# A fused attention and bilinear feed-forward kernel: another PSUM bank for the tail-tail scores in four slots, value products right behind them, and later key transposes

## Chip, cores, metric

One Trainium2 chip (trn2), one core. The metric is the device time of one execution in microseconds (us); lower is better. The runs of one kernel lie within 0.1 to 0.75 per cent of each other; differences below one per cent are therefore judged by traces as well as by times. All runs told here are fast, at a granted TensorE clock of 0.994 to 1.0.

## The reference

Attention with a relative position bias for 8 batches of 8 heads (576 positions, 64 wide); its output is the input of a bilinear feed-forward network of width 1536.

```python
def attn(q, k, v, bias_table):               # q, k, v: (8, 8, 576, 64)
    scores = q @ k.T / 8 + bias_table[bucket(|i - j|)]
    return softmax(scores) @ v
def ffn(x, w_a, w_b, w_out):                 # x: (4608, 512), w_a, w_b: (512, 1536)
    return ((x @ w_a) * (x @ w_b)) @ w_out
```

## The kernel before

The kernel schedules by hand. It works in slots: slot `s` computes the scores of one pair of heads and, beside it, the value products of pair `s - 1` and some "units" of the feed-forward part: `a` and `b` (one 128x512 block of `x @ w_a` or `x @ w_b`) and `o` (output). The 576 positions are 4 blocks of 128 and a tail of 64, so there are main scores, tail scores (`qkt`) and tail-tail scores (`qktt`). PSUM has eight banks: four for scores, one each named AV and TR, and a ring of two named FF.

```python
    ps_av = ctx.enter_context(tc.tile_pool(name="ps_av", bufs=1, space=bass.MemoryType.PSUM))
    ps_tr = ctx.enter_context(tc.tile_pool(name="ps_tr", bufs=1, space=bass.MemoryType.PSUM))
    ps_ff = ctx.enter_context(tc.tile_pool(name="ps_ff", bufs=2, space=bass.MemoryType.PSUM))
    ...
    def qk_tail(p):                                        # TensorE: qkt, then qktt
        ...
        pt = bank(AV if wide(p) else TR, FP32, f"qktt{p}")
        ...
    def ex_tail(p):                                        # ScalarE: exp of qktt, then of qkt
    def run(s, us):          # main scores of slot s and four units, as two half-array streams;
        ...                  # the units' banks: FF and AV, then FF and TR
    def put_in(us, where):   # a plain unit: 4 matmuls, then its eviction
        ...                  # an 'a' ends on ScalarE (L544), a 'b' with a product on VectorE (L548)
    def turns(s):                                          # transposes by DMA, for the next batch
        b = s // 4 + 1
        if 2 < b < B and s % 4 < 3:
            turn(b, "qkt"[s % 4])                          # queries, keys, then the tails QTt and KTt
    ...
            # slots from 9 on; o = output units, rest = plain 'a' and 'b' units
            first = o[0:1] or rest[0:1]
            rest = rest if o else rest[1:]
            steps += [lambda: run(s, four), lambda: qk_tail(s), lambda: put_in(first, FF), lambda: ex_tail(s),
                      lambda: mul(s, 0)] + TQ + X(o[1:2]) + [lambda: mul(s, 1)]
            steps += TK + X(o[2:]) if o else []
            steps += [A(0, 1, 2), N(0)]                    # value products in AV, normalisation
            steps += [] if o else TK
            steps += X(rest[0:1]) + [lambda: mul(s, 2), A(3, 4), N(3), lambda: t_x(s - 1), lambda: turns(s)]
            steps += X(rest[1:2]) + [lambda: mul(s, 3), lambda: mul_tail(s)]
```

`mul` is the multiplication by the exponentials of the bias (VectorE), `N` the normalisation (VectorE), `TQ` and `TK` are transposes on TensorE with their copies out on VectorE.

The softmax here doesn't subtract the row's maximum and nothing guards it: scores larger than these inputs give would overflow.

Of the kernel before, what the change touches and what calls it, by code (L numbers as in the profile page):

```python
# [13 lines left out]
def kernel(  # L14
# [12 lines left out]
    FP32 = mybir.dt.float32  # L27
# [92 lines left out]
    def wide(p):  # L120
        return p >= R4
# [158 lines left out]
    TR = (ps_tr, "tr")  # L280
# [3 lines left out]
    def bank(where, dt, name):  # L284
        return where[0].tile([128, 512 if dt is FP32 else 1024], dt, tag=where[1], name=name)
# [65 lines left out]
    def qk(p, t0):  # L351
        qk1(p, t0)
        qk1(p, t0 + 1)

    def ex(p, t):
        ps = st[p]["ps", t]
        at = atp.tile([128, 2, SM], BF16, tag="at", name=f"at{p}_{t}")
        nc.scalar.activation(out=at[:, :, :], in_=ps[:, :, :], func=ACTF.Exp, scale=scale)  # L358
        st[p]["at", t] = at

    def mul(p, t):
        at, w = st[p]["at", t], W_sb[p % 4]
        lo, hi = max(0, 128 * (t - 1)), min(SM, 128 * (t + 2))
        y = 383 - (lo - 128 * (t - 1))
        z = y - (hi - lo)
        nc.vector.tensor_tensor(out=at[:, :, lo:hi], in0=at[:, :, lo:hi],  # L366
                                in1=w[:, :, y:(None if z < 0 else z):-1], op=MULT)

    def qk_tail(p):
        ps = ps_sc.tile([128, 2, 512], FP32, tag="sc", name=f"qkt{p}")  # L370
        if wide(p):
            for t in range(NM):
                for hh in range(2):
                    r = slice(64 * hh, 64 * hh + 64)
                    nc.tensor.matmul(out=ps[:, hh, ST * t:ST * t + ST], lhsT=kT_(p, t)[r, :],  # L375
                                     rhs=qTt_(p)[r, ST * hh:ST * hh + ST], start=True, stop=True)
            for x in range(2):
                nc.tensor.matmul(out=ps[:, x, 256:512], lhsT=kTt_(p), rhs=qT_(p)[:, 2 * x:2 * x + 2, :],  # L378
                                 start=True, stop=True)
        for t in range(NM if not wide(p) else 0):  # L380
            nc.tensor.matmul(
                out=ps[:, 0, :].rearrange("p (h t c) -> p h t c", h=2, t=NM)[:, :, t, :],
                lhsT=kT_(p, t), rhs=qTt_(p), start=True, stop=True)
        if not wide(p):
            nc.tensor.matmul(out=ps[:, 1, :], lhsT=kTt_(p), rhs=qT_(p), start=True, stop=True)
        pt = bank(AV if wide(p) else TR, FP32, f"qktt{p}")
        for hh in range(2):
            nc.tensor.matmul(out=pt[:, 0:ST], lhsT=kTt_(p), rhs=qTt_(p)[:, ST * hh:ST * hh + ST],
                             start=(hh == 0), stop=(hh == 1))
        st[p]["ps"] = (ps, pt)  # L390

    def ex_tail(p):
        ps, pt = st[p]["ps"]
        at = att_sb[p % 2]
        nc.scalar.activation(out=at[:, 1024:1024 + ST], in_=pt[:, 0:ST], func=ACTF.Exp, scale=scale)  # L395
        if not wide(p):
            nc.scalar.activation(out=at[:, 0:1024].rearrange("p (a x) -> p a x", a=2),
                                 in_=ps[:, :, :], func=ACTF.Exp, scale=scale)
        else:
            nc.scalar.activation(out=at[:, 0:1024].rearrange("p (y a x) -> p a y x", y=2, a=2),  # L400
                                 in_=ps[:, :, :].rearrange("p a (y x) -> p a y x", y=2),
                                 func=ACTF.Exp, scale=scale)
# [218 lines left out]
    def put_in(us, where):  # L621
        nonlocal here
        for u in us:
            here = where
            for x in u_mms(u):
                mm(x)
            here = None
            u_end(u)
# [21 lines left out]
    def run(s, us):  # L650
        u, v_ = [sorted(x, reverse=True) for x in (us[0:2], us[2:4])]
        u, v_ = list(zip(u, (FF, AV))), list(zip(v_, (FF, TR)))
        qk1(s, 0)
        ex(s, 0)
        got0 = begin(*u)
        qk1(s, 1)
        ex(s, 1)
        got1 = begin(*v_)
        qk1(s, 2)
        ex(s, 2)  # L660
        end(*u, got0)
        qk1(s, 3)
        ex(s, 3)
        end(*v_, got1)
# [156 lines left out]
    def turns(s):  # L821
        b = s // 4 + 1
        if 2 < b < B and s % 4 < 3:
            turn(b, "qkt"[s % 4])
# [12 lines left out]
    for s in range(4, NP + 1):  # L837
        new = s < NP
        U = "unit"
        A = lambda *jq: (lambda: [av(s - 1, j, AV if j < 3 or s == NP else TR) for j in jq])  # L840
        N = lambda j: (lambda: norm(s - 1, j))
        steps = []
        if s == 4:
            steps += [U, U, lambda: qk1(4, 0), lambda: ex(4, 0), lambda: qk1(4, 1), U, lambda: ex(4, 1),
                      lambda: qk1(4, 2), U, lambda: ex(4, 2), lambda: qk1(4, 3), lambda: ex(4, 3),
                      lambda: mul(4, 0), U, tails4, U, lambda: qk_tail(4), lambda: ex_tail(4),
                      lambda: mul(4, 1), U, lambda: mul(4, 2), U, lambda: mul(4, 3),
                      lambda: mul_tail(4), U, lambda: t_q(5, TR), lambda: c_q(5), U,
                      lambda: t_k(5, AV), lambda: c_k(5), U, U]
        elif new and s >= R4:  # L850
            e = early((s + 1) // 4)
            n_in, n_out = plan.get(s, (6, 3))
            four, rest, o = take(ins, 4), take(ins, n_in - 4), take(outs, n_out)
            X = lambda us: [lambda: put_in(us, FF)]
            TQ = [lambda: t_q(s + 1, TR), lambda: c_q(s + 1)] if e else []
            TK = [lambda: t_k(s + 1, TR), lambda: c_k(s + 1)] if e else []
            first = o[0:1] or rest[0:1]
            rest = rest if o else rest[1:]
            steps += [lambda: run(s, four), lambda: qk_tail(s), lambda: put_in(first, FF), lambda: ex_tail(s),
                      lambda: mul(s, 0)] + TQ + X(o[1:2]) + [lambda: mul(s, 1)]  # L860
            steps += TK + X(o[2:]) if o else []
            steps += [A(0, 1, 2), N(0)]
            steps += [] if o else TK
            steps += X(rest[0:1]) + [lambda: mul(s, 2), A(3, 4), N(3), lambda: t_x(s - 1), lambda: turns(s)]
            steps += X(rest[1:2]) + [lambda: mul(s, 3), lambda: mul_tail(s)]
        elif new:
            X1 = [lambda: t_x(s - 1, TR), lambda: c_x(s - 1), lambda: turns(s)]
            steps += [lambda: qk(s, 0), lambda: ex(s, 0), U, lambda: ex(s, 1), A(0, 1, 2), N(0), U,
                      lambda: mul(s, 0), A(3, 4), N(3), U, lambda: mul(s, 1)]
            steps += X1 if s == R4 - 1 else []  # L870
            steps += [lambda: qk(s, 2), lambda: ex(s, 2), U, lambda: t_q(s + 1, TR), lambda: c_q(s + 1),
                      lambda: ex(s, 3), U, lambda: mul(s, 2), lambda: t_k(s + 1, AV), lambda: c_k(s + 1),
                      U, lambda: mul(s, 3), lambda: qk_tail(s), lambda: ex_tail(s), U]
            steps += X1 if s < R4 - 1 else []
            steps += [U, lambda: mul_tail(s), U]
        else:
            steps += [U, A(0, 1, 2), N(0), U, U, A(3, 4), N(3), U, U, lambda: t_x(s - 1, AV),
                      lambda: c_x(s - 1), U, U, U, U]
        quota = quotas.get(s, 9)
        if s == NP:  # L880
            ring3 = True
            c = ins[0][1]
            units = [u for u in outs if u[1] < c] + [u for u in ins if u[1] == c]
            units += [u for u in outs if u[1] == c]
            for d in range(c + 1, NCH):
                units += [u for x in (ins, outs) for u in x if u[1] == d]
            nxt = 0
        seen, put = 0, 0
        nu = sum(1 for x in steps if x is U)
        for x in steps:  # L890
            if x is U:
                seen += 1
                n = (quota * seen + nu - 1) // nu - put
                put_units(n)
                put += n
            else:
                x()
        b = s // 4 + 1
        if new and s % 4 == 2 and b + 1 < B:
            load_qkt(b + 1)  # L900
        if new and 2 <= b < B:
            if s % 4 == 0:
                load_v(b)
                if b % 2 == 0:
                    load_vt(b, 2)
# [31 lines left out]
```

## Time and profile before

| | before |
|---|---|
| median of 3 runs at first, 4 with one beside the changed kernel | 414.95 us, 414.91 us |
| span of the profiled run | 413.9 us |
| TensorE busy | 399.2 us, 96% |
| TensorE start to start, 512 columns | 0.216 us |

How to read it: a core whose TensorE is busy nearly throughout gains only where TensorE stands still, so all that follows is about gaps of 0.1 to 1 us between matmul starts. The prediction shows those lines. "Lost" below always means: the start of a matmul, less the start of the one before it, less what that one costs (columns / 2.4 plus 2.5 ns, which fits the 0.216 us and, for 128 and 65 columns, the 0.056 and 0.029 of this trace). One more view of the kernel before matters for what came: the tile KTt, the transposed tail keys of the next batch, from the query by tile.

```profile
L378 PE MATMUL qkt<-QTb,KTt x2: 272/278/283, 114.8 to 114.9; 128*128 128x256 bf16 x2
...
L331 SPq DMA_TRANSPOSE KTt<-ktl x1: 1371/1371/1371, 106.7 to 106.7; - x1
...
DMA to landing us min/median/max: 6.2/6.2/6.2
```

The transpose was issued at 106.71 us and landed at 112.86; its reader, the tail scores of slot 12, started at 114.83. In this trace there were 2 us to spare.

### The profile page before, as it was taken

To read this page: it belongs to the slowest core of one execution; us is meant where nothing else is said; L and a number is where in the kernel's file an instruction comes from. 1 tells how busy PE (TensorE), PEld (TensorE's weight loads), DVE (VectorE), ACT (ScalarE), POOL (GpSimd) and SP (SyncE) were. 2 spreads that over 40 slices of the span, in tenths; PEclk is the share of its full clock that TensorE was granted. 3 is DMA by queue.
4 is the path that set the end of the run, shared out by engine and by line. 5 is a ranking of instruction groups with operands and counts; after the bars stand their busy time and mean duration, and the time that the engine had idled before them with its cause. 6 is when DMAs were issued, how large, how long until landed. Compare 5 with 4: busy or idle time off the path is not lost.

```text
span 413.9 us, 9454 instructions
## 1 busy us (share of the span) xinstructions
PE 399.2 (96%) x3831; PEld 218.9 (53%) x3890; DVE 201.0 (49%) x531; ACT 244.0 (59%) x345; POOL 119.6 (29%) x161
## 2 busy tenths in 40 slices
PE   8799999999999999999999999999999999999996
PEld 3574555566656555555555555555555544444443
DVE  4685666656465444644455455555544330430330
ACT  4997476676887666766666666666666222322321
POOL 9897848904455006600550030000000000000000
PEclk9999999999999999999999999999999999999999
DMA  9999999999979939992899249421111202002004
GB/s 159 189 155 178 158 159 150 180 147 125 140 54 169 164 47 85 152 143 63 78 170 145 64 61 122 92 65 42 35 35 41 65 2 102 2 0 102 2 1 101
DMA packets 164940, 40.83 MB, mean 99 GB/s; under 512 B 155320, under 2 KB 160224, under 8 KB 164896
## 3 DMA queue, kind: packets, MB, share of 16 engines
q0 software_dynamic: 110448, 18.75, 63.9%
q1 hardware_dynamic: 53168, 21.03, 27.7%
q8 instruction: 30, 0.49, 0.5%
q10 hardware_dynamic: 1280, 0.43, 0.5%
q14 instruction: 14, 0.11, 0.1%
HBM read 38.77 MB, written 9.45 MB: 116 GB/s over the span
## 4 chain that ended last, share of the span: by engine, by line
PE 82%; DMA 10%; POOL 4%; issue 2%; DVE 1%; ACT 1%; POOLq 0%; DVEq 0%
PE pa L538 21%; PE po L538 21%; PE pb L538 20%; PE av L432 7%; PE qk L347 6%; DMA wb<-in_moe_w_b_dram 4%; DMA kn<-in_k_dram 4%; PE av L423 2%; DMA vm<-in_v_dram 2%; PE qkt L378 2%; PE qkt L375 1%; PE po L555 1%; POOL qn L134 1%; POOL kn L134 1%; DVE XG L469 1%
## 5 line engine op out<-in xcount | busy, mean ns | idle before, releaser
L538 PE MATMUL pb<-xn,wb 64*128 64x512 bf16 (+1 forms) x592 | 156.6, 377 | 1.3
L538 PE MATMUL pa<-xn,wa 128*128 128x512 bf16 (+1 forms) x609 | 157.2, 377 | 0.7 <-DVE XG L469 0.3
L358 ACT ACTIVATE at<-qk 128x1024 bf16<-128x1024 f32 x128 | 129.3, 1026 | 38.6 <-PE qk L347 36.3
L544 ACT ACTIVATE ha<-pa 128x512 f32<-128x512 f32 x108 | 64.8, 600 | 61.8 <-PE pa L538 60.7
L538 PEld LDWEIGHTS <-wa 64*128 64x128 bf16 (+1 forms) x616 | 56.6, 96 | 44.3 <-DVE XG L469 2.3
L538 PEld LDWEIGHTS <-wb 64*128 64x128 bf16 (+1 forms) x616 | 56.8, 96 | 41.1 <-issue 1.5
L548 DVE TENSOR_TENSOR g<-pb,ha 128x512 bf16<-128x512 f32 x60 | 41.5, 692 | 65.5 <-PE pb L538 38.3
L366 DVE TENSOR_TENSOR at<-at,W 128x512 bf16<-128x512 bf16 (+1 forms) x128 | 59.4, 483 | 2.3 <-DMA W<-bias_tab 2.1
L128 POOL DMA_DIRECT2D vm<-in_v_dram x32 | 28.2, 918 | 95.1 <-PE av L432 83.5
L573 ACT ACTIVATE ob<-po 128x512 f32<-128x512 f32 x35 | 20.9, 598 | 55.6 <-PE po L538 53.6
L538 PE MATMUL po<-wo,g 128*128 128x512 bf16 x216 | 51.8, 379 | 0.6
L432 PEld LDWEIGHTS <-at 128*128 128x128 bf16 x992 | 39.3, 97 | 8.7 <-issue 3.3
L432 PE MATMUL av<-vm,at 128*128 128x65 bf16 x992 | 42.9, 193 | 0.0
L548 DVE TENSOR_TENSOR q<-pb,ha 128x512 bf16<-128x512 f32 x32 | 22.1, 692 | 41.8 <-ACT ha L544 21.0
L423 PE MATMUL av<-vt,att 128*128 128x130 bf16 x156 | 34.6, 222 | 2.3 <-ACT att L395 2.2
L538 PEld LDWEIGHTS <-g 128*128 128x128 bf16 x228 | 21.5, 98 | 22.9 <-issue 0.7
L468 DVE RECIPROCAL rc<-av 128x6 f32<-128x6 f32 x64 | 12.1, 188 | 44.1 <-PE av L432 43.5
L469 DVE TENSOR_TENSOR XG<-av,rc 128x384 bf16<-128x384 f32 x64 | 31.4, 491 | 2.2
L347 PE MATMUL qk<-QTb,KTb 64*128 64x512 bf16 x160 | 32.0, 379 | 0.0
L128 POOL DMA_DIRECT2D qn<-in_q_dram x28 | 24.3, 911 | 21.7 <-PE trq L296 14.3
L538 PE MATMUL po<-wo,q 128*128 128x512 bf16 x116 | 29.6, 379 | 0.6
L128 POOL DMA_DIRECT2D kn<-in_k_dram x28 | 24.4, 914 | 3.4 <-DMA wb<-in_moe_w_b_dram 1.8
(133 smaller groups left out, 349.2 us busy)
## 6 DMA issues: line engine op xcount, KB each, us to landing
out_dram<-ob SPq DMA_DIRECT2D x32, 256.0 KB, 2.3
vm<-in_v_dram POOLq DMA_DIRECT2D x28, 128.0 KB, 5.5
qn<-in_q_dram POOLq DMA_DIRECT2D x24, 128.0 KB, 8.0
kn<-in_k_dram POOLq DMA_DIRECT2D x24, 128.0 KB, 8.3
wa<-in_moe_w_a_dram POOLq DMA_DIRECT2D x3, 512.0 KB, 7.4
wb<-in_moe_w_b_dram POOLq DMA_DIRECT2D x3, 512.0 KB, 9.5
wo<-in_moe_w_out_dram POOLq DMA_DIRECT2D x1, 1536.0 KB, 13.3
W<-bias_tab POOLq DMA_DIRECT2D x4, 192.0 KB, 5.6
```

Source lines behind the costliest of these rows:

```text
L128: nc.gpsimd.dma_start(out=(vm[b % 2][:, h0:h1, t, 0:Dh] if dst is None else dst[b % 2][:, :].rearrange("p (t h d) -> p t h d", h=H, t=NM)[ ...
L347: nc.tensor.matmul(out=ps[:, hh, :], lhsT=kT_(p, t)[r, :], rhs=qT[r, :, :], start=True, stop=True)
L358: nc.scalar.activation(out=at[:, :, :], in_=ps[:, :, :], func=ACTF.Exp, scale=scale)
L366: nc.vector.tensor_tensor(out=at[:, :, lo:hi], in0=at[:, :, lo:hi], in1=w[:, :, y:(None if z < 0 else z):-1], op=MULT)
L423: nc.tensor.matmul(out=pav[:, slot, :, :], lhsT=x, rhs=vt[b // 2 % 2][:, 4 * i + hp, :, 0:Dh + 1], start=fresh, stop=True, skip_group_chec ...
L432: nc.tensor.matmul(out=pav[:, slot, hh, :], lhsT=x, rhs=vm[i][:, 2 * hp + hh, t, 0:Dh + 1], start=False, stop=True, skip_group_check=True)
L468: nc.vector.reciprocal(out=rc, in_=pav[:, 0:n, :, Dh])
L469: nc.vector.tensor_tensor(out=xg[:, j0:j0 + n, :, :], in0=pav[:, 0:n, :, 0:Dh], in1=rc.unsqueeze(3).to_broadcast([128, n, 2, Dh]), op=MULT)
L538: return nc.tensor.matmul(out=o[:, :], lhsT=w[r, :], rhs=m[r, :], start=first if start is None else start, stop=final if stop is None else ...
L544: nc.scalar.activation(out=ha[:, :], in_=ff.pop(("pa", df))[:, :], func=ACTF.Copy)
L548: nc.vector.tensor_tensor(out=g_sb[c % 2][df][:, :], in0=ff.pop(("pb", df))[:, :], in1=ff.pop(("ha", df))[:, :], op=MULT)
L573: nc.scalar.activation(out=ob[:, :], in_=po[:, :], func=ACTF.Copy)
```

## The change

In the four slots that have no output units (10, 11, 12, 17) the tail-tail scores leave AV for a bank of the FF ring, and the value products, which need AV, follow at once; the plain units move behind. In slots 5 to 8 the key transposes go behind the tail scores; in slot 8 the transposes of the last result go later too. Nothing is added or removed.

```diff
-    def qk_tail(p):
+    def qk_tail(p, where=TR):
...
-        pt = bank(AV if wide(p) else TR, FP32, f"qktt{p}")
+        pt = bank(where, FP32, f"qktt{p}")
...
+            back = [lambda: norm(s - 1, 3), lambda: t_x(s - 1), lambda: turns(s)]
+            steps += [lambda: run(s, four)]
+            if o:
+                (as before, with qk_tail(s, AV), and ex_tail ahead of the first output unit)
+            else:
+                steps += [lambda: qk_tail(s, FF), lambda: ex_tail(s), A(0, 1, 2), N(0), lambda: mul(s, 0)] + TQ
+                early_x = X(rest[0:1]) + TK + X(rest[1:2])
+                steps += (early_x if e else []) + [lambda: mul(s, 1), A(3, 4)] + back + [lambda: mul(s, 2)]
+                steps += ([] if e else early_x) + [lambda: mul(s, 3), lambda: mul_tail(s)]
...
             # slots 5 to 8
-            steps += X1 if s == R4 - 1 else []
             steps += [lambda: qk(s, 2), lambda: ex(s, 2), U, lambda: t_q(s + 1, TR), lambda: c_q(s + 1),
-                      lambda: ex(s, 3), U, lambda: mul(s, 2), lambda: t_k(s + 1, AV), lambda: c_k(s + 1),
-                      U, lambda: mul(s, 3), lambda: qk_tail(s), lambda: ex_tail(s), U]
+                      lambda: ex(s, 3), U, lambda: mul(s, 2)]
+            steps += X1 if s == R4 - 1 else []
+            steps += [U, lambda: mul(s, 3), lambda: qk_tail(s), lambda: ex_tail(s),
+                      lambda: t_k(s + 1, AV), lambda: c_k(s + 1), U]
```

More of the change, by code (lines that the diff above doesn't have):

```diff
@@ L856 @@
             TK = [lambda: t_k(s + 1, TR), lambda: c_k(s + 1)] if e else []
-            first = o[0:1] or rest[0:1]
-            rest = rest if o else rest[1:]
-            steps += [lambda: run(s, four), lambda: qk_tail(s), lambda: put_in(first, FF), lambda: ex_tail(s),
-                      lambda: mul(s, 0)] + TQ + X(o[1:2]) + [lambda: mul(s, 1)]
-            steps += TK + X(o[2:]) if o else []
-            steps += [A(0, 1, 2), N(0)]
-            steps += [] if o else TK
-            steps += X(rest[0:1]) + [lambda: mul(s, 2), A(3, 4), N(3), lambda: t_x(s - 1), lambda: turns(s)]
-            steps += X(rest[1:2]) + [lambda: mul(s, 3), lambda: mul_tail(s)]
+            back = [lambda: norm(s - 1, 3), lambda: t_x(s - 1), lambda: turns(s)]
+            steps += [lambda: run(s, four)]
+            if o:
+                steps += [lambda: qk_tail(s, AV), lambda: ex_tail(s), lambda: put_in(o[0:1], FF), lambda: mul(s, 0)]
+                steps += TQ + X(o[1:2]) + [lambda: mul(s, 1)] + TK + X(o[2:]) + [A(0, 1, 2), N(0)]
+                steps += X(rest[0:1]) + [lambda: mul(s, 2), A(3, 4)] + back
+                steps += X(rest[1:2]) + [lambda: mul(s, 3), lambda: mul_tail(s)]
+            else:
[3 more added lines that the diff above has]
+                steps += ([] if e else early_x) + [lambda: mul(s, 3), lambda: mul_tail(s)]
         elif new:
@@ L869 @@
                       lambda: mul(s, 0), A(3, 4), N(3), U, lambda: mul(s, 1)]
+            steps += [lambda: qk(s, 2), lambda: ex(s, 2), U, lambda: t_q(s + 1, TR), lambda: c_q(s + 1),
+                      lambda: ex(s, 3), U, lambda: mul(s, 2)]
             steps += X1 if s == R4 - 1 else []
-            steps += [lambda: qk(s, 2), lambda: ex(s, 2), U, lambda: t_q(s + 1, TR), lambda: c_q(s + 1),
-                      lambda: ex(s, 3), U, lambda: mul(s, 2), lambda: t_k(s + 1, AV), lambda: c_k(s + 1),
-                      U, lambda: mul(s, 3), lambda: qk_tail(s), lambda: ex_tail(s), U]
+            steps += [U, lambda: mul(s, 3), lambda: qk_tail(s), lambda: ex_tail(s),
+                      lambda: t_k(s + 1, AV), lambda: c_k(s + 1), U]
             steps += X1 if s < R4 - 1 else []
```

## The prediction

> **What bounds the kernel now.** I began with the page: how busy each engine is, and the 40 slices.
>
> ```profile
> PE 399.2 (96%) x3831; PEld 218.9 (53%) x3890; DVE 201.0 (49%) x531; ACT 244.0 (59%) x345; POOL 119.6 (29%) x161
> ...
> PE   8799999999999999999999999999999999999996
> ```
>
> TensorE is busy 96% of 413.9 us; no other engine reaches 60%, and after the third slice no slice of TensorE is below nine tenths. The program order of TensorE therefore sets the time, and this change, which adds and removes no instruction, can win only the moments in which TensorE stands still. Next I read the list of waits, for TensorE alone:
>
> ```profile
> PE av L423 <- ACT att L395: 2.2, 3, 0.8
> ...
> PE trx L495 <- DVE XG L469: 0.7, 3, 0.3
> PE trk L316 <- DMA kn<-in_k_dram: 0.6, 1, 0.6
> ...
> PE pa L538 <- DVE XG L469: 0.3, 1, 0.3
> ```
>
> These are small. Ends of matmuls are modelled, so this list understates the loss; from here on I measure from start to start. A 512-column matmul starts 0.216 us after the one before it, a 128-column one 0.056, a value product 0.030. Gaps of exactly one matmul (0.22) where a group of 4 shows 3 are missing records and cost nothing. The timeline of TensorE in slots 10 and 11:
>
> ```profile
> 97.80 0.39 PE L296 MATMUL trq<-cst_sb,qn 128*128 128x128 bf16 x4
> 98.76 0.22 PE L423 MATMUL av<-vt,att 128*128 128x130 bf16 x1 [0.58 <-ACT att L395]
> ...
> 99.99 1.03 PE L538 MATMUL pb<-xn,wb 128*128 128x512 bf16 x4
> 101.16 0.22 PE L423 MATMUL av<-vt,att 128*128 128x130 bf16 x1
> ...
> 106.62 0.22 PE L388 MATMUL qktt<-KT 128*128 128x64 bf16 x2
> 106.73 1.02 PE L538 MATMUL pa<-xn,wa 128*128 128x512 bf16 x3
> 108.56 0.22 PE L423 MATMUL av<-vt,att 128*128 128x130 bf16 x1 [0.80 <-ACT att L395]
> ```
>
> In slot 11 the unit ends at 106.73+4x0.216=107.6 and the first value product starts at 108.56: 0.96 lost. It waits until the tail-tail scores have been read out of the one AV bank. Slot 10 loses 98.76-(97.80+4x0.056)=0.74, and another 0.31 at 101.16 (TR bank, key copy). Slot 17 loses 0.96 in the same form (value products at 166.54). The reason is on ScalarE and VectorE in slot 11:
>
> ```profile
> 105.84 1.03 ACT L358 ACTIVATE at<-qk 128x1024 bf16<-128x1024 f32 x1
> 106.75 0.62 ACT L544 ACTIVATE ha<-pa 128x512 f32<-128x512 f32 x1
> 107.80 0.60 ACT L544 ACTIVATE ha<-pa 128x512 f32<-128x512 f32 x1 [0.43 <-PE pa L538]
> 108.29 0.22 ACT L395 ACTIVATE att<-qktt 128x64 bf16<-128x64 f32 x1
> ...
> 105.99 0.69 DVE L548 TENSOR_TENSOR q<-pb,ha 128x512 bf16<-128x512 f32 x1 [1.61 <-ACT ha L544]
> ```
>
> The unit that was to hide the exponential stands ahead of it on ScalarE: its own eviction (107.80) waits for the unit's matmuls, and the tail exponential comes after that.
>
> **What the Trainium skill says.** "Perfetto Trace Analysis", section Optimization Strategy: find the gaps on the engine you optimise and what releases them; a bubble that repeats can mean too few PSUM buffers. Agreed: the same AV wait stands in slots 10, 11 and 17. "PSUM — Partial Sum Buffer", section Engine vs sequencer instructions: ScalarE and VectorE queues are strict first in, first out, and matmuls start and complete in program order. Agreed: the 0.22 us exponential sits behind the 0.60 us eviction. "PSUM — Partial Sum Buffer", section PSUM bank collisions: guard by bank, not by address; so 64 columns of scores hold all of AV. "TensorEngine Tiling (Array Packing)", section Key Properties: a change of tiling mode drains TensorE; the trace shows about 0.10 us where 128-row matmuls turn to 64-row ones (slot 11: 101.86). The change keeps these switches.
>
> **The change part by part.** In slots with output units only statements of different engines change places; TensorE, ScalarE and VectorE each keep their order. No gain there (slots 9, 13 to 16, 18 to 31).
>
> *Slots 10, 11, 12, 17.* The scores go into the FF bank of the slot's first 'b' unit, the value products follow at once, and the plain units move behind them.
>
> Slot 11: FF is free when VectorE has multiplied that 'b' unit: 105.99+0.69=106.68. The tail-tail scores now start at 106.62, so they wait about 0.1. The value products need only AV, long free: 0.96-0.1=0.85 gained. The last two groups need TR, freed by the eviction ending 107.37, and come at about 107.8: no wait.
>
> Slot 17: same pattern (VectorE 163.97+0.69=164.66 against scores at 164.61): 0.85.
>
> Slot 12: no wait on the exponential, but the next slot's first 'a' unit in AV waits for the normalisation, which VectorE does after the unit's product and two multiplies by the bias:
>
> ```profile
> 116.25 0.69 DVE L548 TENSOR_TENSOR k<-pb,ha 128x512 bf16<-128x512 f32 x1 [0.68 <-PE pb L538]
> 116.86 0.88 DVE L366 TENSOR_TENSOR at<-at,W 128x512 bf16<-128x512 bf16 x2
> 117.66 0.19 DVE L468 RECIPROCAL rc<-av 128x6 f32<-128x6 f32 x1
> ...
> 118.50 0.39 PE L538 MATMUL pa<-xn,wa 64*128 64x512 bf16 x1 [0.32 <-DVE XG L469]
> ```
>
> This wait also puts the two half-array streams out of step. From a slot's first scores to its last tail-tail score takes 106.68-101.86=4.82 in slot 11, 123.11-117.57=5.54 in slot 13, and 4.95 in slot 12, where it is milder. With the normalisation early all should take 4.82: 0.72+0.13=0.85 gained.
>
> Slot 10 has transposes too. Scores wait 0.15 (FF, 96.88), value products end near 97.95, query transposes 98.2. Then the first unit needs the other FF bank: VectorE 97.60+0.69=98.3, 0.1 lost; it ends 99.2. The key transposes need the query copy out of TR: VectorE goes product (to 98.2), reciprocal 0.23, normalise 0.47, bias multiply 0.33 (start-to-start steps in the trace), copy 0.42, so done at about 99.7: 0.5 lost. The 0.74 and 0.31 come down to about 0.8: 0.25 gained.
>
> *Slots 5 to 8.* Key transposes go behind the tail scores. In slot 7 they wait for keys:
>
> ```profile
> 71.01 0.38 PE L316 MATMUL trk<-cst_sb,kn 128*128 128x128 bf16 x3
> 72.01 0.23 PE L316 MATMUL trk<-cst_sb,kn 128*128 128x128 bf16 x1 [0.62 <-DMA kn<-in_k_dram]
> 72.19 0.39 PE L381 MATMUL qkt<-KT 128*128 128x128 bf16 x4
> ```
>
> That load lands at 71.96 in the trace's landing times, on a queue busy at nine tenths, whatever TensorE does. So only the tail scores (4x0.056+0.216+2x0.03=0.49) move into the wait: 0.5 gained. A key wait of 0.26 in slot 5 (52.5) also goes, but what it saves is waited again at 71.96: nothing.
>
> Slot 8: the transposes of the last result move from before the second scores, where they wait 0.46 for the normalisation (78.16) and then hold the query transposes 0.14, to after the third multiply. In TR they now stand right before the tail scores: the copy out takes 0.52 after a multiply, the tail scores fill 0.44 of it, so I expect a new wait of 0.3. 0.60-0.3=0.3 gained.
>
> Sum: 0.5+0.3+0.25+0.85+0.85+0.85=3.6 us. 414.95-3.6=411.35; I say 411.4.
>
> **Rivals.** (1) The FF bank becomes the bound: the scores wait for VectorE, which comes one step later than ScalarE's eviction of AV. For it: VectorE ends only 0.1 after the scores' start. Against: VectorE has over 1.6 us idle before that product. If each of four slots lost 0.5 more, 413.4. (2) DMA takes the gain: the tail transposes for slot 12 land at 111.56 and 112.86, and the tail scores need them at 114.49 and 114.83; TensorE gets there 2.0 us earlier. For: that leaves no slack if the landing is fixed. Against: they are issued behind the normalisation of slot 10, itself about 0.9 earlier. It would cost up to 1 us: 412.4. (3) All waits vanish, since VectorE's queue is shorter than I reckon: 0.96+0.96+1.05+0.85 in the late slots and 0.5+0.6 in the early: 4.9, 410.0.
>
> **Range and chances.** 8 in 10: 410.4 to 413.0, from a little short of rival 3 to most of rival 1. The whole removable loss is under 5 us, and 2% is 8.3 us, so faster by over 2% is almost impossible; a loss of over 8 us would need a new wait of 2 us in each changed slot, which no queue shows. Runs agreed within 0.35 us.
>
> **What would show it.** Value products right after tail-tail scores in slots 10, 11, 12, 17; no TensorE wait on the tail exponential; tail-tail scores waiting about 0.1 on VectorE in 10, 11, 17; a wait of key transposes on a VectorE copy of about 0.5 in slot 10; slot 13 some 4.82 long to its scores; in slot 7 a key wait near 71.96 after the tail scores; in slot 8 a short wait of the tail-tail scores. It is wrong if slot 18 does not start some 3.6 us earlier, or the stretch after it changes.

## The result, and the profile after

413.07 us median (412.82 to 413.54, 4 runs) against 414.91 (414.62 to 414.97, 4 runs): a ratio of 0.9958 with a 95% interval of 0.9941 to 0.9976. Ratios are the mean time of one kernel's fast runs over that of the other's fast runs of the same rounds, so not quite the ratio of the medians that I quote. The gain is real, 1.84 us by the medians, about half of the 3.6 that I had summed, and the time lies 0.07 above my range. "Within 2%" was right.

The page of the changed kernel has TensorE busy 1.7 us less in a span 2.1 us shorter:

```profile
span 411.8 us, 9455 instructions
...
PE 397.5 (97%) x3831; PEld 215.8 (52%) x3890; DVE 200.9 (49%) x531; ACT 244.0 (59%) x345; POOL 119.5 (29%) x161
```

From TensorE's list of waits after:

```profile
PE qkt L378 <- DMA KTt<-ktl: 0.8, 1, 0.8
...
PE trk L316 <- DVE QT L262: 0.6, 1, 0.6
PE trk L316 <- DMA kn<-in_k_dram: 0.5, 1, 0.5
...
PE pb L538 <- DVE k L548: 0.4, 1, 0.4
...
PE qktt L388 <- DVE xn L262: 0.2, 1, 0.2
```

The wait on the tail exponential, first in the list before, is gone. Of the lines shown, the first and the fourth are waits that the kernel before did not have and that my sum did not contain. The other three it did contain. The timeline of TensorE in slot 11 (first two lines), then in slots 12 and 13:

```profile
105.80 0.22 PE L388 MATMUL qktt<-KT 128*128 128x64 bf16 x2
105.86 0.22 PE L423 MATMUL av<-vt,att 128*128 128x130 bf16 x1
...
112.66 0.28 PE L375 MATMUL qkt<-QTt,KTb 64*128 64x64 bf16 x8
113.70 0.39 PE L378 MATMUL qkt<-QTb,KTt 128*128 128x256 bf16 x2 [0.76 <-DMA KTt<-ktl]
...
118.34 0.37 PE L538 MATMUL pb<-xn,wb 64*128 64x512 bf16 x1 [0.43 <-DVE k L548]
```

The value products start 0.06 after the scores, where 0.96 was lost before. But slot 12 loses 0.92 until KTt has landed (0.09 of it is lost at this place in every slot from 9 to 13, waiting or not), and slot 13 loses 0.59 until a product of VectorE has left an FF bank. How far each slot start moved, from both traces (the first main scores of the slot; differences rounded by themselves):

| slot starts | before | after | moved | length of the slot before it changed by | predicted for that slot |
|---|---|---|---|---|---|
| 8 | 73.92 | 73.42 | -0.50 | (slots 5 to 7) -0.50 | -0.5 |
| 9 | 82.12 | 81.35 | -0.77 | (8) -0.27 | -0.3 |
| 10 | 91.88 | 91.11 | -0.78 | (9) -0.01 | 0 |
| 11 | 101.86 | 100.82 | -1.03 | (10) -0.25 | -0.25 |
| 12 | 110.16 | 108.33 | -1.83 | (11) -0.80 | -0.85 |
| 13 | 117.57 | 116.44 | -1.13 | (12) **+0.70** | -0.13 |
| 14 | 127.34 | 126.12 | -1.22 | (13) **-0.09** | -0.72 |
| 17 | 159.84 | 158.62 | -1.22 | (14 to 16) 0 | 0 |
| 18 | 169.00 | 166.93 | -2.07 | (17) -0.85 | -0.85 |

By the start of slot 19 it is 2.12, and it is 2.11 at the last matmul. All terms of the sum hold but those of slots 12 and 13: together +0.61 instead of -0.85.

**KTt.** The query by tile for the changed kernel:

```profile
L331 SPq DMA_TRANSPOSE KTt<-ktl x1: 1324/1324/1324, 106.0 to 106.0; - x1
...
DMA to landing us min/median/max: 7.6/7.6/7.6
```

Issued 0.70 earlier than before (106.01), it landed 0.79 later (113.65), while TensorE wanted it 2.0 earlier (113.70 less the 0.92 lost, against 114.83).

**The product.** VectorE in slots 12 and 13 of the changed kernel:

```profile
115.08 0.20 DVE L468 RECIPROCAL rc<-av 128x6 f32<-128x6 f32 x1 [1.45 <-PE av L432]
115.31 0.56 DVE L469 TENSOR_TENSOR XG<-av,rc 128x384 bf16<-128x384 f32 x1
115.79 0.89 DVE L366 TENSOR_TENSOR at<-at,W 128x512 bf16<-128x512 bf16 x2
...
117.14 0.55 DVE L366 TENSOR_TENSOR at<-at,W 128x768 bf16<-128x768 bf16 x1
117.61 0.68 DVE L548 TENSOR_TENSOR k<-pb,ha 128x512 bf16<-128x512 f32 x1
```

From 115.08 on it works without a pause, and the product of the unit, whose matmuls are done by 116.4, comes last, ending at 118.29. The product holds the FF bank that slot 13 needs at 117.75. Before the 115.08 line VectorE idles for 1.45 us: there was room, in the wrong place.

Two terms that did come as reckoned: in slot 7 the last key transpose starts at 72.01 as before, now behind the tail scores, and in slot 8 the tail-tail scores wait for a copy out of TR, with 0.34 lost:

```profile
72.01 0.23 PE L316 MATMUL trk<-cst_sb,kn 128*128 128x128 bf16 x1 [0.53 <-DMA kn<-in_k_dram]
...
79.99 0.23 PE L388 MATMUL qktt<-KT 128*128 128x64 bf16 x2 [0.18 <-DVE xn L262]
```

### The profile page after: what moved, and what is told of

The parts are those of the page before. It is cut to its first block, busy times and chain, and to the rows that moved or that the text cites. A ratio compares the mean times of both kernels' runs of the same rounds, so it can differ in the third digit from the quotient of the medians.

```text
span 411.8 us, 9455 instructions
## 1 busy us (share of the span) xinstructions
PE 397.5 (97%) x3831; PEld 215.8 (52%) x3890; DVE 200.9 (49%) x531; ACT 244.0 (59%) x345; POOL 119.5 (29%) x161
## 4 chain that ended last, share of the span: by engine, by line
PE 76%; DMA 13%; POOL 6%; DVE 2%; issue 2%; SPq 1%; ACT 0%; POOLq 0%; ACTq 0%; DVEq 0%
PE po L538 21%; PE pa L538 19%; PE pb L538 19%; PE av L432 7%; PE qk L347 5%; DMA wb<-in_moe_w_b_dram 5%; DMA qn<-in_q_dram 3%; DMA vm<-in_v_dram 2%; DMA KTt<-ktl 2%; PE qkt L378 2%; PE av L423 2%; DMA kn<-in_k_dram 1%; DVE at L366 1%; PE po L555 1%; POOL vt L150 1%
## 5 line engine op out<-in xcount | busy, mean ns | idle before, releaser
L347 PE MATMUL qk<-QTb,KTb 64*128 64x512 bf16 x160 | 31.0, 379 | 0.0
```

What stands on the lines that cost most here:

```text
L347: nc.tensor.matmul(out=ps[:, hh, :], lhsT=kT_(p, t)[r, :], rhs=qT[r, :, :], start=True, stop=True)
```

## The experiments

All outputs are right. Theory: the missing half is the two new waits, each with its own cause. Each call has its own runs of the kernel before (medians 414.79, 414.61 and 415.25 in the three calls), so ratios are the fairer comparison between calls.

### One part alone

**e1**: the kernel before with the part for slots 5 to 8. **e2**: the changed kernel without it.

```diff
 # condensed; e1, on the kernel before (slots 5 to 8 only); e2 is the changed kernel with this undone
-            steps += X1 if s == R4 - 1 else []
...
-  ..., lambda: mul(s, 2), lambda: t_k(s + 1, AV), lambda: c_k(s + 1), U, lambda: mul(s, 3), lambda: qk_tail(s), lambda: ex_tail(s), U]
+  ..., lambda: mul(s, 2)] + (X1 if s == R4 - 1 else [])
+  + [U, lambda: mul(s, 3), lambda: qk_tail(s), lambda: ex_tail(s), lambda: t_k(s + 1, AV), lambda: c_k(s + 1), U]
```

> Only the part for slots 5 to 8, on the kernel before. My step: slot 9 starts 0.8 us earlier (the changed kernel's slot 9 is 0.77 earlier). Theory (the gain of the early slots is real and lasts, as nothing later is short by less than 0.8): 414.9 - 0.8 = 414.1, no wait for KTt in slot 12. Rival (transfers set the later pace and take the early gain back): 414.7 to 415.0, with a DMA wait in slots 10 to 17.

Measured: 414.24 us median of 6, ratio 0.9985 (0.9969 to 1.0002). The size is between theory and rival and its interval just reaches 1, so the times alone don't settle it. In the trace slot 8 is 0.27 shorter, as in the changed kernel, and slot 12 touches the landing of KTt (113.44) with 0.06 lost beyond the 0.09 that this place always costs. But slot 9 starts 1.39 before that of the kernel before here, not the 0.8 of the early part, because the keys of slot 7 landed at 71.34 instead of 71.96; and KTt took 8.13 us from issue to landing, where it took 6.15 in the kernel before. Both together used up the slack, not the early part alone.

> Only the part for slots 10, 11, 12 and 17. Theory A (the transpose KTt lands at a moment fixed by the traffic, 113.65 in the changed kernel's trace, so TensorE arriving 0.8 later waits 0.8 less): wait for KTt 0.0 to 0.2, the wait of pb in slot 13 stays at 0.4 to 0.6, and the time is about as in the changed kernel, 412.8 to 413.3, the early part being worth nothing in it. Rival (the landing follows its issue, which is 0.8 later here): the wait for KTt stays near 0.8 and the time is 413.07 + 0.8 = 413.9.

Measured: 413.66 us, ratio 0.9969 (0.9952 to 0.9986). The stated wait was a miss: it is 1.2, not 0.0 to 0.2. In this trace the keys of slot 7 came early, so slot 9 starts 1.15 before that of the kernel before even without the early part, and slot 12 reaches the tail scores earlier still. KTt landed at 113.69, close to the 113.65 of the changed kernel, but that doesn't tell theory A from the rival: the issue came at 105.61, 0.40 earlier than in the changed kernel and not 0.8 later, and with that kernel's 7.64 us from issue to landing the rival would give 113.25. The time, between the two expectations, decides nothing either. One trace's early slots vary by some tenths with the landing of keys, so a term of the early part can't be read from one trace against another.

### The landing of KTt

**e3** issues the two tail transposes in slot 9, directly behind the keys' (and so for every later batch):

```diff
-        if 2 < b < B and s % 4 < 3:
-            turn(b, "qkt"[s % 4])
+        if 2 < b < B and s % 4 < 2:
+            for what in ("q", "kt")[s % 4]:
+                turn(b, what)
```

> The changed kernel, with the tail transposes QTt and KTt issued in slot 9 right behind KTb, one slot earlier. Theory (slot 12 of the changed kernel loses 0.9 to the landing of KTt and nothing else stands behind that wait): no DMA wait in slot 12, 413.07 - 0.9 = 412.2. Rival (the two transposes now delay KTb or the loads, and the wait turns up again on qk of slot 12 or on another transfer): 412.8 to 413.3, with that wait in the list.

Measured: 411.99 us, ratio 0.9935 (0.9916 to 0.9954), 0.95 us below the changed kernel by ratio (0.0023 of 415). No DMA wait in slot 12; that slot is now 0.12 shorter than in the kernel before, where I had predicted 0.13. The rival falls. (The intervals of the two ratios overlap, so it is the trace that carries this, and e10 repeats it.)

**e8** was to hold the loads of batch 4 back, to see whether they delay KTt:

```diff
-        if new and s % 4 == 2 and b + 1 < B:
+        if new and (s == 11 if b == 3 else s % 4 == 2) and b + 1 < B:
```

> The changed kernel with the loads of batch 4 (queries, keys, tails) started after slot 11 instead of slot 10. Theory (KTt lands late because the loads of batch 4 share the transfer engines with it; its landing stood at 112.9 to 113.7 in five traces whether it was issued at 105.0 or at 106.7): it lands 4 to 6 us after its issue, before 111.5, and the wait in slot 12 goes: 412.2. Rival (the transposes in front of it on its own queue hold it): landing stays 7 to 8 us after the issue, 413.1; or batch 4 comes too late and slot 16 waits.

Measured: 413.17 us, ratio 0.9964. The edit did nothing: GpSimd's instruction order is the same, as no other instruction of that engine stood between, and the loads were again issued from 97.2 on. So it says nothing of either theory, but it repeats the changed kernel on another chip job: 413.17 beside 413.07. **e10** does it properly, with a one-element copy on GpSimd, into a new tile `late`, that needs the last multiply of slot 11:

```diff
+        if s == 11:
+            nc.gpsimd.tensor_copy(out=late[:, :], in_=att_sb[s % 2][0:1, 1024:1025])
+        if new and (s == 11 if b == 3 else s % 4 == 2) and b + 1 < B:
```

> The changed kernel with the loads of batch 4 really held back: e8's edit left the order on the issuing engine as it was, so it was a mere repetition. Here a copy of one element, which waits for the end of slot 11, stands ahead of them. Theory (KTt lands 8 us after its issue because these loads share the transfer engines): it lands 4 to 6 us after its issue, by 111.5, no wait in slot 12, 413.1 - 0.9 = 412.2. Rival (what holds it is its own queue, the four transposes ahead of it): landing stays 7 us or more after the issue, wait of 0.8 or more, 413.1.

Measured: 412.00 us, ratio 0.9921 (0.9906 to 0.9936). The loads start at 109.94, and the query by tile gives for KTt:

```profile
L331 SPq DMA_TRANSPOSE KTt<-ktl x1: 1262/1262/1262, 105.2 to 105.2; - x1
...
DMA to landing us min/median/max: 4.1/4.1/4.1
```

Landed at 109.33, with the same transposes ahead of it on its queue: the rival falls. With the loads in flight it took 6.2 to 8.9 us in every trace in which it was issued between 105.0 and 106.7 (landings 112.86 in the kernel before, 113.14 to 114.96 in the others). In the trace of the kernel before, the last three of its five KTt transposes, with no load in flight, took 2.43 to 2.53 us. So the loads of the next batch are what makes this one late. It does not follow that its landing is fixed, as theory A of e2 and e8's theory have it: in the seven other traces of that range of issue times the landing came 7.64 to 8.87 us after the issue, the earliest issue (105.04, e4) had the earliest landing (113.14), and the 6.15 us of the kernel before is the shortest of the eight. Why it was short there stays open. And the much earlier issue of e3 (98.03) did bring an earlier landing (104.12). That the loads lengthen it (4.1 us without them, 6.2 to 8.9 with them) agrees with the Trainium skill, "DMA: Bandwidth & Descriptors", section Issuing engines are not separate DMA queues: transfers started by different engines run on the same DMA engines and interleave.

### The product in slot 12

**e4**: in slot 12 the value products, the unit, and on VectorE the product before the second normalisation and three multiplies:

```diff
+                if not e and len(rest) == 1 and rest[0][0] == "b":
+                    steps += [A(3, 4)] + early_x + back + [lambda: mul(s, 1), lambda: mul(s, 2)]
+                    steps += [lambda: mul(s, 3), lambda: mul_tail(s)]
+                else:  (as in the changed kernel)
```

> The changed kernel, with slot 12's unit put in right behind the value products and its product ahead of the second normalisation and three of the bias multiplies on VectorE. Theory (the wait of pb in slot 13 is the FF bank held by a product that stands behind four VectorE instructions that could come later): the wait of 0.59 goes, 413.07 - 0.6 = 412.5. Rival (VectorE has simply too much to do there, and the second normalisation now holds TR as long): 413.0 to 413.2, with a wait of pa or pb on the normalisation.

Measured: 413.56 us, ratio 0.9966 (0.9947 to 0.9985): no gain. The wait on the product is gone, but another has come, on TensorE (first line) for `hop`, the one-element copy on VectorE that must read a unit's bank before its second half is added (last line):

```profile
119.03 0.37 PE L538 MATMUL pa<-xn,wa 64*128 64x512 bf16 x1 [0.38 <-DVE hop L640]
```

```profile
117.27 1.35 DVE L366 TENSOR_TENSOR at<-at,W 128x768 bf16<-128x768 bf16 x3
...
118.84 0.39 DVE L640 COPY hop<-pa 1x1 f32<-1x1 f32 x2
```

So the theory as I had put it for e4 falls and its rival is half right: in that stretch VectorE has too much to do in either of the two orders tried. (KTt also cost this trace 1.36 in slot 12, so its time alone would not show a gain; but slot 13 takes 9.77, as in the kernel before, against 9.67 in the changed kernel.) What was tried next was to move work out of the stretch. **e5** (on e3) puts the first two multiplies before the normalisation, into the idle 1.45 us, and the product behind the second normalisation:

```diff
+                if not e and len(rest) == 1 and rest[0][0] == "b":
+                    steps += [lambda: mul(s, 0), lambda: mul(s, 1), A(0, 1, 2), N(0), A(3, 4)] + back + early_x
+                    steps += [lambda: mul(s, 2), lambda: mul(s, 3), lambda: mul_tail(s)]
+                else:  (as in the changed kernel)
```

> The tail transposes in slot 9 as in e3, and in slot 12 VectorE's first two bias multiplies ahead of the normalisation (they fit the 1.45 us in which it idles there), its unit's product right behind the second normalisation. Theory (slot 13's wait is VectorE's order, and e4 only pushed it onto the small copy that guards the bank; work moved into the idle time removes it): no wait over 0.2 in slot 13, start of slot 14 0.6 to 0.7 earlier against slot 12 than in e3, time 411.4, which was my prediction for the change. Rival (VectorE has too much to do between the value products of slot 12 and slot 13 whatever the order): the wait turns up again on another VectorE instruction, 411.9 to 412.1.

Measured: 411.49 us, ratio 0.9918 (0.9902 to 0.9933). VectorE in slot 12:

```profile
112.63 0.88 DVE L366 TENSOR_TENSOR at<-at,W 128x512 bf16<-128x512 bf16 x2
113.43 0.19 DVE L468 RECIPROCAL rc<-av 128x6 f32<-128x6 f32 x1
...
114.87 0.69 DVE L548 TENSOR_TENSOR k<-pb,ha 128x512 bf16<-128x512 f32 x1
```

The multiplies are done before the normalisation can start, and the product follows 1.4 us after it. Slot 13 is 0.70 shorter than in the kernel before; I had predicted 0.72. With both waits removed the kernel takes about what I had predicted for the change, 411.4.

### The bank and the order, one without the other

**e6** keeps the new order and puts the scores back into AV; **e7** keeps the new bank and puts the old order back (a unit between scores and value products).

```diff
 # e6
-                steps += [lambda: qk_tail(s, FF), lambda: ex_tail(s), A(0, 1, 2), N(0), lambda: mul(s, 0)] + TQ
+                steps += [lambda: qk_tail(s, AV), lambda: ex_tail(s), A(0, 1, 2), N(0), lambda: mul(s, 0)] + TQ
 # e7: the steps of the kernel before, with
+            steps += [lambda: run(s, four), lambda: qk_tail(s, None if o else FF), lambda: put_in(first, FF), ...
```

> The changed kernel with the tail-tail scores of slots 10, 11, 12, 17 put back into AV, the new order kept. Theory (the other bank is what lets the value products follow at once): the value products wait for the tail exponential again, 0.6 to 0.8 in slots 10, 11, 17 and 0.4 in slot 12, 2.4 in all; the first two take the place of the wait for KTt (0.9), so the time is 413.07 + 1.5 = 414.6. Rival (the order pays, the bank does not): 412.9 to 413.3.

> The changed kernel with the old order in slots 10, 11, 12, 17 (a unit between tail-tail scores and value products), the scores in FF. Theory (FF is a ring of two, so scores in one bank make the unit behind them wait for the second bank, which VectorE frees after its second product): the unit waits 1.2 to 1.4 in slots 10, 11 and 17 and 0.5 in slot 12, more than the 0.7 to 1.0 that AV cost, so slower than the kernel before by 0.3 to 1.0: 415.2 to 416.0. Rival (the bank alone does it): 412.5 to 413.5, without such a wait.

Measured: e6 415.19 us, ratio 1.0009 (0.9992 to 1.0027); e7 416.48 us, ratio 1.0040 (1.0023 to 1.0056). The two lists of waits (e6, then e7):

```profile
PE av L423 <- ACT att L395: 2.4, 4, 0.7
```

```profile
PE pa L538 <- DVE q L548: 2.4, 2, 1.2
...
PE pa L538 <- DVE g L548: 1.2, 1, 1.2
```

In e6 the value products lose 0.90, 0.82, 0.48 and 0.85 in the four slots; I had 0.6 to 0.8 and 0.4, and some wait for KTt is left besides, so it is 0.6 slower than expected. In e7 the unit behind the scores loses 1.35 in slots 10, 11 and 17: the scores have taken one bank of the ring of two, and the other is free only when VectorE has made its second product. In slot 12 it loses 0.17 only, where I had 0.5. The time of e7 is 0.5 above the expected range; its trace also waited 0.34 for the landing of KTt, which the expectation did not have. Both mechanisms stand; the sizes for slots 10, 11 and 17 were a little low in e6 and right in e7. With either part alone the kernel is no faster than before (e6) or slower (e7), though both runs keep the part for slots 5 to 8; only together do they pay.

### Slot 10

**e9** (on e5) puts slot 10's query copy ahead of the normalisation on VectorE:

```diff
-                    steps += [A(0, 1, 2), N(0), lambda: mul(s, 0)] + TQ
+                    steps += [A(0, 1, 2)] + TQ + [N(0), lambda: mul(s, 0)]
```

> e5 with slot 10's query copy ahead of the normalisation and the first bias multiply on VectorE (its transposes are done early). Theory (the wait of 0.72 of the key transposes in slot 10 is VectorE's order, as I sized it at 0.5): that wait goes to under 0.1, 411.5 - 0.7 = 410.8. Rival (the later normalisation or the key copy then holds the last value products as long): 411.4, with a wait of av or of slot 11 on VectorE.

Measured: 410.88 us, ratio 0.9893 (0.9877 to 0.9910). The key transposes follow their unit with nothing lost (0.72 in e5), and 0.11 is lost at the last value products. It is the fastest version here, 1.1% below the kernel before by ratio.

## Why the prediction was wrong

- **What bounds the kernel: right.** No instruction was added, and each us of the gain is a gap of TensorE that closed. Two readings were off, without effect on the sum: the last of the 40 slices is at six tenths, not above nine; and the "nine tenths" at the load of keys is the busy share of the DMA engines, not of one queue.
- **Slots 10, 11 and 17: right** in mechanism and size (-0.25, -0.80, -0.85; the table). e6 shows that the bank is the reason, e7 that the order is needed with it. In slot 10 the key transposes lost 0.73, where I had 0.5, but other waits there came out smaller, so the term holds.
- **Slots 5 to 8: right in mechanism; the size is in part luck.** The pair of traces has -0.77 against -0.8. The 0.3 of slot 8 is sound: that slot takes 8.20 in both traces with the old order and 7.93 in all ten with the new one. The 0.5 of slot 7 rests on keys that landed at 71.96 in both traces of the pair. In e2, with the old order, they landed at 70.81 and only 0.21 was lost, so no more could have been gained; in six of the ten traces with the new order nothing is lost there. By time e1 leaves both terms together at 0.55 us with an interval that touches zero.
- **The failed step, first part:** rival 2, which I set aside with the words that the tail transposes "are issued behind the normalisation of slot 10, itself about 0.9 earlier". The issue did come earlier, by 0.7. But I had taken the time from issue to landing from one trace, 6.15 us, as if the landing would move with the issue; it was 7.64 in the changed kernel, so the landing came 0.8 later while TensorE came 2.0 earlier. At 6.15 it would have landed at 112.16, in time. The longer time isn't the doing of the new order in slots 10 to 12: e1, which keeps the old one, has 8.13. With the loads of batch 4 held back it is 4.1 (e10). I had priced that rival at up to 1 us, and slot 12 lost 0.92 to it, 0.83 more than this place always costs. Removing it gave 0.95 us (e3).
- **The failed step, second part:** in slot 12, "With the normalisation early all should take 4.82". The wait for the normalisation did go. But I had followed only the AV bank, and not where the change puts the unit's product on VectorE: behind two normalisations and three multiplies, with an FF bank in its hand. The new wait of 0.59 took the place of the 0.48 removed, and slot 13 gained 0.09, not 0.72. The one other order tried inside that stretch (e4) only moved the wait; e5, with work moved into the idle time before it, gives the 0.70.
- **The sum:** 3.6, less 0.83 missed in slot 12 and 0.63 in slot 13, is 2.1, which is what the traces show at the last matmul (2.11); the times show 1.84. The profiled run of the kernel before took 415.64, 0.7 more than the median of its timed runs, and lost 0.79 to the keys in slot 7. If the early terms are worth 0.5 rather than 0.8, as e1's times suggest, the sum comes to 1.8; that fits, but isn't shown. My own test, slot 18 some 3.6 earlier, failed at 2.07.

What stays open: how much of the early slots' gain is left in a mean over many runs, as it depends on a landing of keys that moves from run to run (70.35 to 71.96 in the twelve traces); and why KTt took 6.15 us in the one trace of the kernel before and 7.6 to 8.9 in the seven others with loads in flight and an issue at 105.0 to 106.3.

## What to carry to other kernels

When a change pulls the busiest engine earlier, list every transfer that it will reach within the time gained, and don't trust a slack that is read from one trace: the same transpose took 6.15 to 8.87 us from issue to landing beside the same loads, a spread wider than the 2 us of slack that one trace showed. Issue it well ahead, as e3 did, or keep the loads away from it, as e10 did. When a wait is removed by reordering, follow each bank through every instruction that holds it, above all on the engine that now has the longer queue; a product that ends a bank's life belongs before work that nobody waits for. And look for idle time just ahead of the crowded stretch: moving two multiplies there did what e4's reordering of the stretch did not.

## What the Trainium skill lacked or had wrong

- "Advanced Engine Details and Errata", section X-Bar Transpose (TRN2), gives a bandwidth and says that transposes are as fast as regular DMAs; neither it nor "DMA: Bandwidth & Descriptors" says what one small transpose takes from issue to landing beside loads. Here one of 128 x 512 two-byte elements took 2.4 to 2.5 us with no load in flight (later batches of the kernel before), 4.1 us with the loads held back (e10), and 5.8 (e5) to 8.9 us (e7) beside them.
- "Perfetto Trace Analysis", section Optimizing Tensor Performance, advises rotating independent groups through different banks. It lacks the other side: a small result put into a ring of two banks made the group behind it wait 1.35 us for the second bank (e7), more than the 0.74 to 0.96 us wait that it was to remove.
- "Perfetto Trace Analysis", section Optimization Strategy, says to make dependencies start sooner or complete faster. It lacks that the engine gained on then runs into the next dependency: of 3.6 us reckoned, 1.46 did not come in the two slots in which TensorE met waits that did not exist before.
